# Attention begun on the first 512 rows: eight heads on four key blocks with their sums kept, the rest of norm, K and V made beside it

## Chip, cores, metric

One core of one Trainium2 chip. The metric is device time in microseconds (us) of the slowest core, here the only one; the figure quoted for a kernel is the median of its fast runs. "Span" is the time from the first to the last instruction in one profiled execution; it was 1.8 to 2.1 us below that execution's time in the profiled executions quoted here. The "granted clock" is the profile's record of TensorE's clock as a share of full speed (here 1.00 or, halved, 0.50), and PSUM is the memory that matmuls write to.

## The reference

Two layers; each is attention with 32 heads of 16 columns on 2048 rows of 512, then an MLP of width 1792, both with a norm ahead and a residual. Weights are the same in both layers. Inputs and output are bfloat16.

```python
def attention(x, wqkv, wo):                 # x: 1 x 2048 x 512, H = 32, Dh = 16
    q, k, v = split_heads(x @ wqkv)
    scores = einsum("bhqd,bhkd->bhqk", q, k) * Dh ** -0.5
    o = einsum("bhqk,bhkd->bhqd", softmax(scores), v)
    return merge_heads(o) @ wo

for layer in range(2):
    x = x + attention(layernorm(x), wqkv, wo)
    x = x + relu(layernorm(x) @ w1) @ w2
```

Softmax takes 2 x 32 x 2048 x 2048 exponentials. They bound the kernel.

## The kernel before

The program is written in slots. One slot is one set of scores (three blocks of 128 keys x 512 queries, "wide", 1536 columns), the exponential of them on ScalarE, and the product with V of an earlier slot. In some slots VectorE takes the third block over with integer and polynomial steps, so that ScalarE has a "narrow" exponential of 1024 columns. A segment is one lane of four heads (t, of 8) on one group of 512 query rows (j, of 4). All other matmuls (Q, K, V, output projection, MLP) are "fillings" put between, through one PSUM bank, with a model of the engines' times deciding where. Key blocks are 128 rows, so 16 of them make the sequence. The pieces of code below are cut and condensed.

The start: four rounds in a row before any exponential.

```python
for j in range(NQS):                        # four groups of 512 rows
    tag = ("ln1", 0, j)
    for i in range(TPC): ln_stats(tag, j, i)
    ln_rstd(tag)
    # ... j == 0: masks
    for i in range(TPC):
        ln_apply(tag, j, i)
        pt = ln_transpose(tag, i)
        nc.scalar.copy(out=xnT[j][:, :, i * P : (i + 1) * P], in_=pt)
    k_fin(0, 0, j, plain(k_mms(0, j)))
    # ... j == 0: the first Q
    for kb in range(j * TPC, (j + 1) * TPC):
        nc.scalar.copy(out=v_out(0, kb), in_=v_in(plain(v_mms(kb))))
```

The segments: layer 0 runs each segment over all 16 key blocks. Layer 1 already splits the segments of its first 512 rows, since the last rows of layer 0 come late: twelve key blocks with the sums stored, then the last four with the sums loaded.

```python
for j in range(NQS):
    for T in range(4): add_run(0, j, T, range(NKB), False, False)
for T in range(NACC // 2): add_run(1, 0, T, range(NKB - TPC), False, True)      # store
for T in range(NACC // 2): add_run(1, 0, T, range(NKB - TPC, NKB), True, False) # load
```

The end of a segment: the sums leave PSUM (`u`), and the reciprocal of the softmax denominators is made by three small transfers on one queue, so that VectorE computes 128x16 values and not 128x512.

```python
def copy():
    if sg["load"]: nc.vector.tensor_add(out=u[:], in0=acc[t], in1=ps_o[:])
    else:          nc.vector.tensor_copy(out=u[:], in_=ps_o[:])
    mark(("po",))                               # PSUM output bank is free
    if not last:
        nc.sync.dma_start(out=c[:], in_=sums)   # c<-u, 8 KB
        mark(("c", n), lag=2600.0)              # when the schedule counts on it
def recip():
    nc.vector.reciprocal(out=c[:], in_=c[:])
    nc.sync.dma_start(out=sums, in_=c[:])       # u<-c, 8 KB
    nc.sync.dma_start(out=r[:], in_=...)        # r<-u, 256 KB, 32 copies of each row
```

The tail uses seven PSUM banks in rotation, but the banks lie in three tiles, and a wait is for a whole tile:

```python
def bank():
    if not wide[0]: return ps_f[:]
    n = bank_no[0] % 7
    bank_no[0] += 1
    if n == 6: return ps_f[:]
    return ps_s[n // W][:, n % W, :]            # W = 3
```

The softmax here doesn't subtract the row's maximum and nothing guards it: scores larger than these inputs give would overflow.

Of the kernel before, what the change touches and what calls it, by code (L numbers as in the profile page):

```python
# [21 lines left out]
def kernel(  # L22
# [82 lines left out]
    xn2T = sb([P, NDC, QS], BF16, "xn2T")  # L105
    ht = [sb([P, QS], BF16, f"ht{ft}") for ft in range(NF)]
    ot = [sb([P, QS], BF16, f"ot{t}") for t in range(NT)]
# [3 lines left out]
    de = sb([P, 2, QS], BF16, "de")  # L111
    acc = [x[:, k, :] for x in [dm, dy] + dis for k in range(2)]
    ebuf = [sb([P, W, QS], BF16, f"e{n}") for n in range(NE)]
    qbuf = [[sb([P, QS], BF16, f"q{n}_{e}") for e in range(2)] for n in range(2)]
# [16 lines left out]
    wq_src = A_wqkv[:, :].rearrange("(c p) f -> p c f", p=P)  # L131
    for tt in range(4):
        nc.sync.dma_start(out=x_t[tt][:], in_=x_flat[tt * P : (tt + 1) * P, :])
    nc.scalar.dma_start(out=wqkv[:, :, D : 2 * D], in_=wq_src[:, :, D : 2 * D])
    nc.scalar.dma_start(out=wqkv[:, :, 2 * D : 3 * D], in_=wq_src[:, :, 2 * D : 3 * D])
    for tt in range(4, NTT):
        nc.sync.dma_start(out=x_t[tt][:], in_=x_flat[tt * P : (tt + 1) * P, :])
    nc.scalar.dma_start(out=wqkv[:, :, 0:D], in_=wq_src[:, :, 0:D])
    nc.sync.dma_start(out=wo[:], in_=A_wo[:, :].rearrange("(c p) f -> p c f", p=P))
    nc.sync.dma_start(out=w2[:], in_=B_w2[:, :].rearrange("(c p) f -> p c f", p=P))  # L140

    nc.gpsimd.memset(warm[:], 0.0)
    nc.scalar.activation(out=warm[:], in_=warm[:], func=ACTF.Exp)
    make_identity(nc, ident[:])
# [189 lines left out]

    def mm_group(mms, fin, makes, deps, per=2, cost=690, after=None):

        hold = {}
        pieces = []
        n = len(mms)
        for a in range(0, n, per):  # L340

            def piece(a=a):
                if a == 0:
                    hold["b"] = bank()
                b = hold["b"]
                for i in range(a, min(a + per, n)):
                    lhsT, rhs = mms[i]
                    nc.tensor.matmul(b, lhsT, rhs, start=(i == 0), stop=(i == n - 1))  # L348
                if a + per >= n:
                    put_evac(cost, lambda: fin(b))  # L350
                    if after:
                        after()

            pieces.append((min(per, n - a), piece))
        return group(pieces, makes, deps)
# [54 lines left out]
    def ln_rows(tag, j, i):  # L410
# [3 lines left out]
        prev = ln_seq[ln_seq.index(tag) - 1]  # L414
        task(750, lambda: ln_stats(tag, j, i), [("st", tag, i)])
        if i == TPC - 1:
# [105 lines left out]
    def h_group(l, j, ft, war):  # L522
        n = ((l * NQS + j) * NF + ft) % NW1

        def fin(b):
            if wide[0] and ft % 2:
                nc.scalar.activation(out=ht[ft][:], in_=b, func=ACTF.Relu)
            else:
                nc.vector.tensor_scalar(  # L529
                    out=ht[ft][:], in0=b, scalar1=0.0, scalar2=None, op0=ALU.max  # L530
                )
# [53 lines left out]

    def add_run(l, j, T, kbs, load, store):
        n = len(runs)
        runs.append((l, j, T))
        for e in range(2):
            segs.append(  # L590
                {
                    "l": l, "j": j, "t": 2 * T + e, "e": e, "T": T, "kbs": kbs, "n": n,
                    "load": load, "store": store, "begun": set(),
                }
            )

    for j in range(NQS):
        for T in range(4):
            add_run(0, j, T, range(NKB), False, False)
    early = range(NKB - TPC)  # L600
    late = range(NKB - TPC, NKB)
    for T in range(NACC // 2):
        add_run(1, 0, T, early, False, True)
    for T in range(NACC // 2):
        add_run(1, 0, T, late, True, False)
    for T in range(NACC // 2, 4):
        add_run(1, 0, T, range(NKB), False, False)
    for j in range(1, NQS):
        for T in range(4):
            add_run(1, j, T, range(NKB), False, False)  # L610

    norm_no = [0]

    def finish_segment(sg, last):
        l, j, t, e = sg["l"], sg["j"], sg["t"], sg["e"]
        if sg["store"]:
            musts.append(
                (690, now_pe[0] + PE_TO_DVE,
                 lambda: (nc.vector.tensor_copy(out=acc[t], in_=ps_o[:]), mark(("po",))))
            )  # L620
# [9 lines left out]
        def copy():  # L630
            if sg["load"]:
                nc.vector.tensor_add(out=u[:], in0=acc[t], in1=ps_o[:])  # L632
            else:
# [150 lines left out]

    for j in range(NQS):
        tag = ("ln1", 0, j)
        for i in range(TPC):
            ln_stats(tag, j, i)
        ln_rstd(tag)
        if j == 0:  # L790
            for e in range(2):
                nc.vector.tensor_reduce(
                    out=mask[e][:],
                    in_=ident[:].rearrange("p (g e d) -> p e g d", g=4, e=2)[:, e],
                    op=ALU.add, axis=mybir.AxisListType.XY,
                )
            for e in range(2):
                nc.vector.tensor_scalar(
                    out=qmask[e][:], in0=mask[e][:], scalar1=SCALE * LOG2E * UNIT, scalar2=None,
                    op0=ALU.mult,  # L800
                )
        for i in range(TPC):
            ln_apply(tag, j, i)
            pt = ln_transpose(tag, i)
            nc.scalar.copy(out=xnT[j][:, :, i * P : (i + 1) * P], in_=pt)  # L805
            mark(("xnT", tag, i))

        def plain(mms):
            b = bank()
            for i, (lhsT, rhs) in enumerate(mms):  # L810
                nc.tensor.matmul(b, lhsT, rhs, start=(i == 0), stop=(i == len(mms) - 1))  # L811
            return b

        k_fin(0, 0, j, plain(k_mms(0, j)))
        if j == 0:
            urgent.append(q_group(None, 0, 0, 0, 0))
            run_all()
        for kb in range(j * TPC, (j + 1) * TPC):
            nc.scalar.copy(out=v_out(0, kb), in_=v_in(plain(v_mms(kb))))
            mark(("v", 0, kb))  # L820
    for T in range(1, 4):
        work.extend(k_group(0, T, j) for j in range(NQS))
    for tag in [("ln1", 0, NQS - 1)]:
        assert ln_seq[-1] == tag

# [6 lines left out]
    recents = [[], []]  # L832
    exp_end = {-1: 0.0, 0: 0.0}
    pair_at = None
    now_dve[0] = 0.0
    while blocks:
# [16 lines left out]
        sg, kb, g = now[-1]  # L853
        pace = 3.0 if sg["store"] or sg["load"] else max(todo / max(rest - 6.0, 6.0), 0.5)
        owed[0] = min(owed[0] + pace, 6.0) if todo else 0.0
# [21 lines left out]
        half = None  # L877
        if len(now) == W and now[0][0] is sg and not (sg["load"] or sg["store"]):
            r = (kb * 4 + g - 2) // W
            if pair_at is not None:  # L880
                half = 1 if r == pair_at + 2 else None
            elif len(pairs) < 2:
                queued = sum(t["cost"] for t in dve_q if "chain" in t)
# [82 lines left out]
```

## Time and profile before

| | before |
|---|---|
| median of 3 runs | 1879.19 us (1876.68 to 1881.48) |
| profiled span, mean granted clock | 1876.4 us, 0.979 |
| until the first exponential | 67.9 us |
| exponentials on ScalarE | 1725.4 us in 1366 |
| idle of ScalarE before them | 14.5 us |
| after the last one (tail) | 68.6 us |

The four last rows add up to the span. That is the whole accounting: anything that is not in one of these four terms lies beside the exponentials and costs nothing. The lines that they come from are in the prediction.

### The profile page before, as it was taken

The numbers are of one execution on the slowest core, as the hardware profiler recorded it, in microseconds if no ns is written. First come the engines' busy times: TensorE is split into PE (matmuls) and PEld (weight loads), VectorE is DVE, ScalarE is ACT, GpSimd is POOL, SyncE is SP. The second block draws the span as 40 slices with busy tenths as digits, with TensorE's granted clock in tenths as the row PEclk, the third lists the DMA queues.
The fourth block names the chain that finished last, engine by engine and source line by source line (L and its number), as shares of the span: only waits on it lengthen the run. The fifth ranks groups of instructions, "written<-read, shape, count | busy, mean of one in ns | idle before, by whom it ended". The sixth has DMA issues, their size and how long they took to land.

```text
span 1876.4 us, 29319 instructions
## 1 busy us (share of the span) xinstructions
PE 1617.2 (86%) x12546; PEld 517.2 (28%) x12712; DVE 1244.0 (66%) x1864; ACT 1749.2 (93%) x1407; POOL 2.4 (0%) x35
## 2 busy tenths in 40 slices
PE   4788888899888998899899978888889888889966
PEld 2222222222222222222223222222222222222222
DVE  4677767868877786967642322786568768796672
ACT  2699999999999999999899998999999999999950
POOL 0000000000000000000000000000000000000000
PEclk8899999999999999999899998999999999999998
DMA  4000000110001100011001001011000110001101
GB/s 140 1 7 12 13 12 8 23 43 12 8 13 35 27 10 13 13 38 24 11 6 40 1 7 32 12 27 38 21 16 7 35 32 16 13 13 41 26 16 39
DMA packets 92742, 42.24 MB, mean 23 GB/s; under 512 B 76612, under 2 KB 84548, under 8 KB 92612
## 3 DMA queue, kind: packets, MB, share of 16 engines
q1 hardware_dynamic: 91028, 38.79, 9.1%
q8 instruction: 99, 1.62, 0.4%
q10 hardware_dynamic: 1584, 1.57, 0.2%
q14 instruction: 31, 0.25, 0.0%
HBM read 20.71 MB, written 2.10 MB: 12 GB/s over the span
## 4 chain that ended last, share of the span: by engine, by line
ACT 84%; PE 10%; DVE 4%; DMA 2%; issue 1%; SPq 0%; DVEq 0%
ACT e L894 83%; PE ps_s L871 3%; PE ps_o L685 2%; PE ps_f L348 2%; PE ps_s L348 2%; PE ps_s L811 1%; DMA c<-u 1%; DVE stats L367 0%; ACT xnT L805 0%; PE ps_s L404 0%; DMA r<-u 0%; DVE q L484 0%; DVE x L545 0%; DMA x<-in_A_x_dram 0%; DVE ht L529 0%
## 5 line engine op out<-in xcount | busy, mean ns | idle before, releaser
L894 ACT ACTIVATE e<-ps_s 128x1536 bf16<-128x1536 f32 (+1 forms) x1366 | 1725.4, 1552 | 14.5 <-PE ps_s L871 13.4
L871 PE MATMUL ps_s<-q,ktp 32*128 32x512 bf16 x6276 | 702.5, 384 | 170.2 <-ACT e L894 140.0
L685 PE MATMUL ps_o<-e,vaug 128*32 128x512 bf16 x3830 | 545.3, 393 | 7.2 <-DVE u L632 3.3
L871 PEld LDWEIGHTS <-ktp 32*128 32x128 bf16 x6276 | 224.9, 92 | 624.9 <-issue 548.1
L685 PEld LDWEIGHTS <-vaug 128*32 128x32 bf16 x4628 | 166.2, 93 | 455.6 <-issue 426.0
L726 DVE TENSOR_SCALAR di<-ps_s 128x512 int32<-128x512 f32 x266 | 182.9, 688 | 103.6 <-PE ps_s L871 101.2
L756 DVE SCALAR_TENSOR_TENSOR de<-dy,di 128x1024 bf16<-128x1024 f32 x133 | 162.6, 1223 | 7.2
L756 DVE SCALAR_TENSOR_TENSOR dy<-dm 128x1024 f32<-128x1024 f32 x133 | 162.5, 1222 | 2.9
L756 DVE SCALAR_TENSOR_TENSOR dy<-dy,dm 128x1024 f32<-128x1024 f32 x133 | 162.4, 1221 | 2.6
L529 DVE TENSOR_SCALAR ht<-ps_f 128x512 bf16<-128x512 f32 x99 | 68.2, 689 | 101.1 <-PE ps_f L348 100.6
L348 PE MATMUL ps_f<-w,ht 128*128 128x512 bf16 x365 | 110.1, 383 | 6.0 <-issue 4.8
L348 PE MATMUL ps_f<-xn2T,w 128*128 128x512 bf16 x353 | 107.8, 382 | 6.4 <-issue 3.0
L645 DVE SCALAR_TENSOR_TENSOR ot<-u,mask,r 128x512 bf16<-128x512 f32 (+1 forms) x67 | 48.1, 718 | 81.3 <-DMA r<-u 81.1
L685 PE MATMUL ps_o<-de,vaug 128*32 128x512 bf16 x532 | 94.6, 382 | 0.0
L750 DVE TENSOR_SCALAR di<-di 128x1024 int32<-128x1024 int32 x133 | 91.8, 690 | 2.9
L750 DVE TENSOR_SCALAR dm<-di 128x1024 int32<-128x1024 int32 x133 | 91.5, 688 | 1.5
L348 PE MATMUL ps_f<-xnT,wqkv 128*128 128x512 bf16 x210 | 67.2, 388 | 6.1 <-issue 4.5
L484 DVE TENSOR_SCALAR q<-ps_f,qmask 128x512 bf16<-128x512 f32 x70 | 50.2, 743 | 28.0 <-PE ps_f L348 27.5
L685 PE MATMUL ps_o<-di,vaug 128*32 128x512 bf16 x266 | 66.2, 391 | 0.0
L348 PE MATMUL ps_f<-wo,ot 128*128 128x512 bf16 x199 | 61.0, 384 | 1.6 <-issue 1.4
L634 DVE COPY u<-ps_o 128x512 f32<-128x512 f32 x56 | 38.6, 690 | 28.8 <-PE ps_o L685 28.4
L545 DVE TENSOR_TENSOR x<-x,ps_f 128x512 bf16<-128x512 bf16 x29 | 19.9, 685 | 54.6 <-PE ps_f L348 54.1
(67 smaller groups left out, 485.5 us busy)
## 6 DMA issues: line engine op xcount, KB each, us to landing
r<-u SPq DMA_DIRECT2D x63, 256.0 KB
w<-in_B_w_dram SPq DMA_DIRECT2D x112, 128.0 KB
x<-in_A_x_dram SPq DMA_DIRECT2D x16, 128.0 KB
out_dram<-x SPq DMA_DIRECT2D x16, 128.0 KB
w<-in_B_w_dram SPq DMA_DIRECT2D x1, 1792.0 KB
wqkv<-in_A_wqkv_dram ACTq DMA_DIRECT2D x3, 512.0 KB
c<-u SPq DMA_DIRECT2D x63, 8.0 KB
u<-c SPq DMA_DIRECT2D x63, 8.0 KB
```

The costliest lines, as they stand in the source:

```text
L348: nc.tensor.matmul(b, lhsT, rhs, start=(i == 0), stop=(i == n - 1))
L484: nc.vector.tensor_scalar(out=qbuf[n % 2][e][:], in0=b, scalar1=qmask[e][:, 0:1], scalar2=None, op0=ALU.mult,)
L529: nc.vector.tensor_scalar(out=ht[ft][:], in0=b, scalar1=0.0, scalar2=None, op0=ALU.max)
L545: nc.vector.tensor_add(out=x_t[tt][:], in0=x_t[tt][:], in1=b)
L634: nc.vector.tensor_copy(out=u[:], in_=ps_o[:])
L645: nc.vector.scalar_tensor_tensor(out=ot[t][:, a : a + w], in0=u[:, a : a + w], scalar=mask[e][:, 0:1], in1=r[:, a : a + w], op0=ALU.mult, ...
L685: nc.tensor.matmul(ps_o[32 * g : 32 * g + 32, :], vaug[sg["l"]][kb][:, 4 * sg["T"] + g, 2 * e : 2 * e + 32], rhs, start=g not in sg["begun ...
L726: first = nc.vector.tensor_scalar(out=di[:, half, :].bitcast(I32), in0=src, scalar1=EXP_BIAS, scalar2=0.0, op0=ALU.add, op1=ALU.max,)
L750: nc.vector.tensor_scalar(out=out[:].bitcast(I32), in0=di[:].bitcast(I32), scalar1=keep, scalar2=put, op0=ALU.bitwise_and, op1=ALU.bitwise_or,
L756: nc.vector.scalar_tensor_tensor(out=out[:], in0=x[:], scalar=c, in1=y[:], op0=ALU.add, op1=ALU.mult)
L871: nc.tensor.matmul(b[:, w, :], kt[32 * g : 32 * g + 32, kc : kc + P], qbuf[sg["n"] % 2][sg["e"]][32 * g : 32 * g + 32, :], start=True, sto ...
L894: ex = nc.scalar.activation(out=eb[:, :m, :], in_=b[:, :m, :], func=ACTF.Exp, scale=1.0 / (LOG2E * UNIT),)
```

## The change

Attention should begin as soon as the first 512 rows have their norm, K and V. Layer 0 gets the split that layer 1 has: all eight segments of the first 512 query rows go over the four key blocks that exist, with their sums stored in tiles that are free then; later the same eight segments go over the other twelve. The norm, transposes, K and V of the other 1536 rows become fillings. The first loads are reordered (x first, on two queues), idle matmuls are put ahead to have TensorE's clock up, no pairs go to VectorE until all sixteen K tiles of layer 0 exist, and fillings come in pieces of one matmul instead of two.

```diff
+    load_x(nc.sync, (0, 2))
+    load_x(nc.scalar, (1, 3))
+    nc.scalar.activation(out=warm[:], in_=warm[:], func=ACTF.Exp)
+    load_w(nc.sync, D)                     # K; then Q on scalar, x 4-7, V, x 8-15
...
-    def mm_group(mms, fin, makes, deps, per=2, cost=690, after=None):
+    def mm_group(mms, fin, makes, deps, per=1, cost=690, after=None):
...
+        early = range(TPC if l == 0 else NKB - TPC)
+        late = range(len(early), NKB)
+        sums = acc0 if l == 0 else acc
+            add_run(l, 0, T, early, store=sums)
...
+            add_run(l, 0, T, late, load=sums)
...
+    idle_matmuls(18)
+    # statistics, root, four transposes of the first 512 rows, one idle matmul after each,
+    # masks, three statistics of the next rows, K(0), Q(0), V(0), V(1); then:
+    work.extend(v_group(0, kb) for kb in range(2, TPC))
+    for j in range(1, NQS):
+        # ... ln_rows, k_group(0, j, 0), ln_groups, k_group(0, 0, j), v_groups as fillings
...
-            elif len(pairs) < 2:
+            elif len(pairs) < 2 and not any(key not in made for key in first_layer):
```

(Cut to its core; the rest renames buffers and sets the model's clock for the new start.)

## The prediction

> **What bounds the kernel now.** I read the page's busy shares first, then the instructions of ScalarE's one big group laid over time, then the timelines of the two ends.
>
> ```profile
> PE 1617.2 (86%) x12546; PEld 517.2 (28%) x12712; DVE 1244.0 (66%) x1864; ACT 1749.2 (93%) x1407; POOL 2.4 (0%) x35
> ACT  2699999999999999999899998999999999999950
> ```
>
> ScalarE is 93% busy, and its row of slices is 9 everywhere but at the two ends and, slightly, in the middle. The costliest groups say what it does:
>
> ```profile
> L894 ACT ACTIVATE e<-ps_s 128x1536 bf16<-128x1536 f32 (+1 forms) x1366 | 1725.4, 1552 | 14.5 <-PE ps_s L871 13.4
> L726 DVE TENSOR_SCALAR di<-ps_s 128x512 int32<-128x512 f32 x266 | 182.9, 688 | 103.6 <-PE ps_s L871 101.2
> ```
>
> Of 1749.2 us, 1725.4 are softmax exponentials, with only 14.5 us of idle before them. The second line is the first step of the exponentials VectorE takes over: 266 blocks of 128x512 in 133 pairs. Each such block shortens one ScalarE exponential from 1536 columns to 1024. The timelines of the ends:
>
> ```profile
> 3.04 0.69 DVE L367 BATCH_NORM_STATS2 stats<-x 128x6 f32<-128x512 bf16 x1 [3.04 <-DMA x<-in_A_x_dram]
> 5.00 0.69 DVE L367 BATCH_NORM_STATS2 stats<-x 128x6 f32<-128x512 bf16 x1 [1.05 <-DMA x<-in_A_x_dram]
> 6.77 0.69 DVE L367 BATCH_NORM_STATS2 stats<-x 128x6 f32<-128x512 bf16 x1 [0.86 <-DMA x<-in_A_x_dram]
> ...
> 15.97 1.87 PE L811 MATMUL ps_s<-xnT,wqkv 128*128 128x512 bf16 x4 [0.73 <-ACT xnT L805]
> ...
> 46.06 1.02 PE L811 MATMUL ps_s<-xnT,wqkv 128*128 128x512 bf16 x4 [0.67 <-ACT xnT L805]
> ...
> 67.89 7.91 ACT L894 ACTIVATE e<-ps_s 128x1024 bf16<-128x1024 f32 x7
> ```
>
> The first exponential begins at 67.89 us. Before it lie four serial rounds (one per 512 rows) of norm, transpose, K and V, in which ScalarE was busy only 19.7 us with copies. The last exponential ends at 1807.8, and 68.6 us of last output projection, norm and MLP follow. So the span is 67.9 + (1725.4 + 14.5) + 68.6 = 1876.4 us. The timed median, 1879.2, is 2.8 above that span.
>
> The idle 14.5 us matter for the rivals. Two stretches of the table of windows hold most of it (columns: stretch, length, busy PE, PEld, DVE, ACT, POOL with counts, granted clock, DMA):
>
> ```profile
> 904.00:908.00 4.00, 4.00 (x25) 0.74 (x22) 3.06 (x4) 2.77 (x3) 0.00 (x0) 0.50 0.02 4
> 1156.00:1160.00 4.00, 4.00 (x27) 0.74 (x24) 0.42 (x2) 2.99 (x3) 0.00 (x0) 0.50 0.19 39
> ```
>
> TensorE's clock is half there, and TensorE is full while ScalarE waits for scores. Just before, TensorE had stood for one VectorE copy of the output sums (2.9 us at 1150).
>
> **What the Trainium skill says.** "Perfetto Trace Analysis", section Identifying the Most-Contended Engine: for ScalarE, occupancy is a fair measure of how near the roofline is. The trace agrees: 100.00 busy in most 100 us stretches. "TensorE: Matmul & The Clock Gate", Part 1: The HAM clock gate: the clock is halved by default and released by roughly 3.4 us of activity; 512 columns then start every 215.7 ns, not 426.7. The trace agrees: four K matmuls took 1.87 us at 15.97 and 1.02 at 46.06. "Trainium Kernel Development and Optimization", section Key Constraints: queues of different engines share the same 16 DMA engines, so more queues save only issue time. The trace fits: with a 512 KB weight transfer issued at 0.73 beside them, the second and third x tiles came only at 5.0 and 6.8, while the engines moved about 380 GB/s.
>
> **The change, part by part.**
>
> *1. Earlier start.* Attention now begins when 512 rows have norm, K for T=0, Q and two V blocks. I walk its path with the durations above.
> - All four x tiles are issued first, on two queues. 512 KB at 380 GB/s is 1.4 us, so with the first at 3.0 none should hold VectorE. Statistics take about 0.79 us a tile back to back, ending near 6.3 (8.5 before).
> - The reciprocal root is 12 small operations of about 0.2 us, to 8.7.
> - Normalised rows, transposes and copies: the transposes still wait for the copy before them, since banks share a tile (the trace shows that wait, 0.67 us). Four rounds of 0.4 + 0.5 to 0.6 take it to 12.9. The 18 idle matmuls are there to have the clock full by then: 8 cold ones at 0.43 and 10 warm at 0.22 end near 7.
> - K 1.0, its copy on ScalarE 0.65, Q 1.0 (it waits for that copy): 15.6. VectorE has put the masks and three statistics of the next rows before Q's copies (0.55 + 2.4), so is free at 15.9. Two Q copies end at 17.3. V0 and V1 end on TensorE at the same time.
> - Scores 0.4, and ScalarE's copy of V1: first exponential at about 18.0.
>
> 67.9 - 18.0 = **49.9 us saved**. The 19.7 us of ScalarE copies before also leave (14 of 16 transposes' copies and 14 of 16 V copies go to VectorE or beside attention), but they lay inside those 67.9, so they are not counted again.
>
> *2. Exponentials given back.* The first runs (eight segments of four key blocks, 128 blocks) take no VectorE pairs, nor does any segment until all sixteen K tiles of layer 0 exist. The instruction order of the changed kernel has 1131 exponentials of 1536 columns and 234 of 1024, against 1099 and 266: 32 blocks return to ScalarE. In bins of 128 blocks the first two fall from 12 and 10 narrow ones to 0 and 2; the other 12 are lost here and there by the packing. The form means differ by 1637 - 1206 = 431 ns, so **+13.8 us** of ScalarE, all on the path.
>
> *3. Work beside attention.* The norm of 1536 rows, their transposes, K and 14 V blocks now run under the exponentials. A wide exponential starts every 1.343 us (14 of them in 18.91 us, the last lasting 1.45). TensorE per slot: scores and values about 0.22 each (row groups run at once), two switches near 0.1, and two to four filling matmuls of 0.22: 1.1 to 1.5 us. It just fits. VectorE from the first exponential to the last V copy sums to 47 us of instructions against 57 slots, 77 us: it fits. But two places do not:
> - Right after the start VectorE runs a statistic (0.8) and the root chain (2.4) before the next Q's two copies (1.4). The single filling bank is held meanwhile; V2 stands behind it in TensorE's order, before the values and scores of slot 4. Scores come near 23.4 where 22.1 was needed: 1.4 us.
> - Slots 53 to 58: transposes, K and four V blocks of the last rows are forced in a row, each through one bank and one VectorE copy: about 1 us for K, 1 for the V blocks.
>
> Any pause there may halve the clock, and a slot with two fillings then needs about 2 x 0.9 + 0.2 = 2.0 us, over 1.343, for several slots. I put 2.5 us on that. Together **+6 us** of idle.
>
> *4. The rest.* Four more Q groups and eight more hand-overs of sums fall on TensorE and VectorE, beside the exponentials. Smaller filling pieces (one matmul, not two) should not delay scores more than before. Layer 1 keeps its short runs, so I keep the 14.5 us and the 68.6 us tail.
>
> Sum: 18.0 + (1725.4 + 13.8) + (14.5 + 6.0) + 68.6 = 1846.3 us of span; plus 2.8 for the timed median: 1849, and I take **1848 us**, 1.7% less, as Part 1 may run a little shorter than my walk.
>
> **Rivals.**
> - *TensorE becomes the bound of the first 100 us.* For: 1.1 to 1.5 us of work per 1.343 us slot, one filling bank, and the half clock that followed hand-over pauses at 900 and 1150 now has eight more hand-overs to arise from. Against: clock was 1.00 in every 100 us stretch from 100 to 900. It would cost some 10 to 15 us more: about 1860.
> - *No added stalls, and smoother layer 1.* The smaller pieces and the altered statistic cost (860 for 750) look tuned. If the early stalls are 1 to 2 us and the half-clock stretches near 900 and 1150 lose half their 13 us, the time is about 1838, over 2% faster.
> - *The start is held by the weights or by a cold clock.* The Q weights are issued after the table load on ScalarE's queue. For: 2 MB of x and 1.5 MB of weights compete. Against: at 380 GB/s even all 3.6 MB are in by about 12, and Q's matmul is at 14.6. If the idle matmuls fail to warm it, K, Q and V lose about 0.9 us each: first exponential at 21, about 1851.
> - *VectorE loses nothing by offloading less and the returned blocks cost nothing.* That needs ScalarE to have slack; 100.00 busy speaks against. It would give 1834.
>
> **Range and chances.** Start is good to 2 us, the returned blocks to half a microsecond, early stalls to about 4, layer 1 to about 5; added as squares about 7 us, and 1.28 of that is 9. I widen upwards for cold-clock episodes: 1837 to 1860. The 2% line is 1841.6, almost one such spread below my value: faster 0.18, within 2% 0.81, slower 0.01.
>
> **What would show it.** First exponential at 16 to 20 us; x statistics back to back from about 3 us with no DMA waits; the group of exponentials with about 1739 us busy and about 20 us idle before them; the narrow form counted 234; no half clock beyond a few microseconds before 120; tail near 68.6. I am wrong if the idle before exponentials passes 30 or falls under 12, or if the first exponential is later than 22.

## The result, and the profile after

| | runs | median us |
|---|---|---|
| before, same comparison | 4 | 1878.15 |
| after | 4 | 1855.68 (1848.99 to 1862.37) |

The ratio is 0.9878, 95% interval 0.9838 to 0.9917: 1.2% less time, within the 2% line. Ratios here are the mean time of one kernel's fast runs over the mean of the other's fast runs of the same rounds, so they are not quite the ratio of the medians quoted. Executions over 1.5% slower than the fastest of the same kernel are left out of the means.

The page after, lines that answer to those of before:

```profile
PE 1660.1 (89%) x12509; PEld 521.9 (28%) x12509; DVE 1170.9 (63%) x1796; ACT 1749.7 (94%) x1380; POOL 2.4 (0%) x35
ACT  6999998999999999999999998999999999999940
L926 ACT ACTIVATE e<-ps_s 128x1536 bf16<-128x1536 f32 (+1 forms) x1366 | 1741.2, 1588 | 28.9 <-PE ps_s L903 27.9
L737 DVE TENSOR_SCALAR di<-ps_s 128x512 int32<-128x512 f32 x234 | 160.8, 688 | 101.2 <-PE ps_s L903 99.8
```

The first slice of ScalarE went from 2 to 6, the exponentials grew from 1725.4 to 1741.2 us, VectorE's share of them fell from 266 blocks to 234, and the idle before exponentials doubled, to 28.9 us.

Its timeline at the start (start, length, engine, line, operation, shapes, count, and in brackets the idle before and what ended it):

```profile
3.26 0.69 DVE L379 BATCH_NORM_STATS2 stats<-x 128x6 f32<-128x512 bf16 x1 [2.14 <-DMA x<-in_A_x_dram]
4.09 0.66 DVE L379 BATCH_NORM_STATS2 stats<-x 128x6 f32<-128x512 bf16 x1
...
13.26 1.02 PE L832 MATMUL ps_s<-xnT,wqkv 128*128 128x512 bf16 x4 [0.39 <-DVE mask L816]
...
18.22 4.14 ACT L926 ACTIVATE e<-ps_s 128x1536 bf16<-128x1536 f32 x3
23.80 9.51 ACT L926 ACTIVATE e<-ps_s 128x1536 bf16<-128x1536 f32 x7 [1.43 <-PE ps_s L903]
```

After the first tile no statistic waits for a transfer, K runs warm, the first exponential is at 18.22 us, and the fourth waits 1.43 us. The walk in the prediction had 18.0 and 1.4.

This profiled execution was the slowest of the four (1862.37 us). The other three were 5 to 13 us shorter, so one look is not enough to account for the kernel. The same kernel again as a control: 1852.7 us (1852.48 to 1853.85, 5 runs), ratio 0.9846 [0.9833, 0.9858]. (One run of the kernel before there took 3272.52 us; it counts as slow and is in no ratio.) The sum in four terms, us:

| term | before | predicted | control | first profile after |
|---|---|---|---|---|
| first exponential | 67.9 | 18.0 | 20.6 | 18.2 |
| exponentials | 1725.4 | 1739.2 | 1739.2 | 1741.2 |
| idle before them | 14.5 | 20.5 | 21.4 | 28.9 |
| tail | 68.6 | 68.6 | 70.7 | 72.2 |
| span | 1876.4 | 1846.3 | 1851.9 | 1860.6 |

The control's group line, for the second and third row:

```profile
L926 ACT ACTIVATE e<-ps_s 128x1536 bf16<-128x1536 f32 (+1 forms) x1366 | 1739.2, 1592 | 21.4 <-PE ps_s L903 20.6
```

The 21.4 us are all gaps before exponentials; 20.6 of them are waits for scores, and the split that follows is of these. Four questions follow. Why did the start reach 18.2 once and 20.6 in the control? Why is the tail longer, when nothing in it was changed? Which part of the change pays and which costs? And what are the 13.6 us of the control's idle that lie between 890 and 1210 us (6.3 lie before 130, 0.6 between), which the kernel before has too (12.7)?

### The profile page after: what moved, and what is told of

The parts are those of the page before. It is cut to its first block, busy times and chain, and to the rows that moved or that the text cites. A ratio compares the mean times of both kernels' runs of the same rounds, so it can differ in the third digit from the quotient of the medians.

```text
span 1860.6 us, 28967 instructions
## 1 busy us (share of the span) xinstructions
PE 1660.1 (89%) x12509; PEld 521.9 (28%) x12509; DVE 1170.9 (63%) x1796; ACT 1749.7 (94%) x1380; POOL 2.4 (0%) x35
## 4 chain that ended last, share of the span: by engine, by line
ACT 84%; PE 10%; DVE 3%; DMA 2%; issue 0%; SPq 0%; DVEq 0%
ACT e L926 84%; PE ps_s L903 4%; PE ps_o L696 2%; PE ps_s L360 2%; PE ps_f L360 1%; DMA c<-u 1%; DVE stats L379 0%; DMA r<-u 0%; DMA wqkv<-in_A_wqkv_dram 0%; DVE ht L542 0%; DVE q L497 0%; DVE vaug L490 0%; DVE ot L656 0%; DVE r L678 0%; DMA u<-c 0%
## 5 line engine op out<-in xcount | busy, mean ns | idle before, releaser
L926 ACT ACTIVATE e<-ps_s 128x1536 bf16<-128x1536 f32 (+1 forms) x1366 | 1741.2, 1588 | 28.9 <-PE ps_s L903 27.9
L737 DVE TENSOR_SCALAR di<-ps_s 128x512 int32<-128x512 f32 x234 | 160.8, 688 | 101.2 <-PE ps_s L903 99.8
L767 DVE SCALAR_TENSOR_TENSOR de<-dy,di 128x1024 bf16<-128x1024 f32 x117 | 143.1, 1223 | 8.9 <-PE ps_o L696 2.5
L767 DVE SCALAR_TENSOR_TENSOR dy<-dm 128x1024 f32<-128x1024 f32 x117 | 142.9, 1221 | 2.4
L767 DVE SCALAR_TENSOR_TENSOR dy<-dy,dm 128x1024 f32<-128x1024 f32 x117 | 142.8, 1220 | 2.1
L360 PE MATMUL ps_f<-xn2T,w 128*128 128x512 bf16 x400 | 122.5, 383 | 3.4 <-DVE ht L542 0.6
L360 PE MATMUL ps_f<-w,ht 128*128 128x512 bf16 x392 | 123.3, 385 | 0.5
L360 PE MATMUL ps_f<-xnT,wqkv 128*128 128x512 bf16 x280 | 88.8, 392 | 4.2 <-DVE vaug L490 1.4
L360 PEld LDWEIGHTS <-w 128*128 128x128 bf16 x448 | 36.2, 98 | 73.4 <-issue 59.3
L360 PEld LDWEIGHTS <-ht 128*128 128x128 bf16 x448 | 34.5, 97 | 70.1 <-issue 57.0
```

Of the source, the lines that this page charges most:

```text
L360: nc.tensor.matmul(b, lhsT, rhs, start=(i == 0), stop=(i == n - 1))
L737: first = nc.vector.tensor_scalar(out=di[:, half, :].bitcast(I32), in0=src, scalar1=EXP_BIAS, scalar2=0.0, op0=ALU.add, op1=ALU.max,)
L767: nc.vector.scalar_tensor_tensor(out=out[:], in0=x[:], scalar=c, in1=y[:], op0=ALU.add, op1=ALU.mult)
L926: ex = nc.scalar.activation(out=eb[:, :m, :], in_=b[:, :m, :], func=ACTF.Exp, scale=1.0 / (LOG2E * UNIT),)
```

## The experiments

Twelve kernels ran, on three chips; the kernel before ran beside them, with medians of 1881 to 1883 us. All results were correct. Unless said otherwise an edit is to the changed kernel. Where a first exponential, tail or idle is quoted, it is from the one profiled execution.

**1. The tail: one more turn of the banks.** In the kernel before, the program asks for a bank 37 times before the tail, 37 mod 7 = 2; after the change 8 times, 8 mod 7 = 1. Then the first two output projections fall into one PSUM tile. TensorE's timeline of the tail in the control, the changed kernel run again (as told above):

```profile
1793.17 5.17 PE L360 MATMUL ps_s<-wo,ot 128*128 128x512 bf16 x16 [3.73 <-DVE x L515]
```

The same stretch in this experiment:

```profile
1788.94 4.02 PE L360 MATMUL ps_s<-wo,ot 128*128 128x512 bf16 x9 [1.41 <-DVE ot L656]
1793.88 1.89 PE L360 MATMUL ps_s<-wo,ot 128*128 128x512 bf16 x8 [0.92 <-DVE x L515]
```

```diff
     wide[0] = True
+    bank_no[0] = 2
     run_all()
```

> Edit: before the tail the bank counter is set to 2, where the kernel before happened to stand; in the changed kernel it stands at 1. Theory (the tail grew from 68.6 to 72.2 us because the first two output projections now fall into banks of one tile, so the second waits for VectorE's addition of the first): from the end of the last exponential to the end of the span 68.6 us, within 0.5, and the time 3.6 us (0.2%) lower than the changed kernel. Rival (the tail is longer only because the clock was halved there): still about 72 us whenever the clock row of the tail is as low, and no wait for the addition removed.

Measured: 1851.32 us (1850.04 to 1861.52, 5 runs), ratio 0.9845 [0.9822, 0.9869]; tail 68.6 us. In the control the second projection stands 3.73 us until VectorE has added the first one to x (`DVE x L515`); with the edit nine matmuls go through in one stretch, and the wait is 0.92, as in the kernel before. The clock is halved for part of the tail in both, as before the change; its first half-clock stretch is 6.8 us with the edit and 10.2 in the control. So the control's extra 2.1 us of tail is what the rotation's phase cost. Experiments 9 and 12, with the same edit, have tails of 68.6 and 68.9. In time alone it is not seen: the ratios of this kernel and the control are 0.9845 and 0.9846. (The first profile of the changed kernel has the same wait of 3.73 and a tail of 72.2; its first half-clock stretch is 13.7 us, and the sixteen matmuls take 6.41 us, not 5.17.)

**2. No idle matmuls.**

```diff
     def idle_matmuls(n):
-        for _ in range(n):
+        for _ in range(0):
```

> Edit: no idle matmuls at the start (22 matmuls left out). Theory (they warm the clock for the start): the first exponential begins 2 to 3.5 us later than 18.2, with K, Q and V at 1.87 us per four matmuls instead of 1.02, and the time is 2 to 4 us higher than the changed kernel. Rival (warming is worth nothing, the path is set by VectorE's statistics and Q copies): first exponential within 1 us of 18.2.

Measured: 1853.23 us (1849.52 to 1853.71, 4 runs), ratio 0.9842 [0.9822, 0.9862]; first exponential at 20.54, K 1.87 us. The control, which has them, has the same. The control's timeline on TensorE:

```profile
1.19 5.61 PE L799 MATMUL ps_o<-e 128*128 128x512 bf16 x18 [1.19 <-DVE e L144]
9.80 0.40 PE L416 MATMUL ps_s<-ident,xn 128*128 128x128 bf16 x4 [3.00 <-DVE xn L407]
...
14.23 1.87 PE L832 MATMUL ps_s<-xnT,wqkv 128*128 128x512 bf16 x4 [0.18 <-DVE mask L816]
```

And two rows of the control's table of windows (stretch, length, busy PE, PEld, DVE, ACT, POOL with counts, granted clock, DMA):

```profile
10.00:12.00 2.00, 1.16 (x10) 0.43 (x7) 0.70 (x3) 0.59 (x1) 0.00 (x0) 0.80 0.98 325
12.00:14.00 2.00, 1.84 (x10) 1.03 (x10) 0.77 (x3) 0.59 (x1) 0.00 (x0) 0.50 0.68 214
```

The eighteen end at 6.8 us, TensorE rests 3.00 us, and the clock goes to half at about 11.2, 3 us before K. In the first profile of the changed kernel the same eighteen took 7.02 us and ended at 8.2, the rest was 1.24 us, and the clock stayed. So in the control the idle matmuls are worth nothing. The other kernels bear this out: of the ten profiled executions with eighteen idle matmuls, the seven with a rest of 2.26 to 3.53 us before the first transposes went to half clock by 12.1 us, and the three with 1.24, 1.88 and 2.01 us (the first profile and those of experiments 10 and 3) had K at 1.02 us. (A trap: the record of the clock starts late when a kernel begins cold. In experiment 2 it reads 1.00 from 14 to 16 us, though K took 1.87 us at 14.02.)

**3. Fillings in pieces of two matmuls, as before the change.**

```diff
-    def mm_group(mms, fin, makes, deps, per=1, cost=690, after=None):
+    def mm_group(mms, fin, makes, deps, per=2, cost=690, after=None):
```

> Edit: filling pieces of two matmuls again, not one. The build has 252 narrow exponentials where the changed kernel has 234, so 18 blocks go back to VectorE. Theory (the returned blocks cost 0.43 us each on ScalarE's path): ScalarE's exponentials are busy 7.7 us less, about 1733 us, and the time is about 8 us (0.4%) lower if idle stays equal. Rival (the one-matmul pieces pay for themselves by less waiting for scores): idle before the exponentials rises by as much or more, 37 us or over, and the time is equal or higher.

Measured: 1860.54 us (1858.25 to 1874.52, 6 runs), ratio 0.9902 [0.9873, 0.993]. Its group line, in its slowest run:

```profile
L926 ACT ACTIVATE e<-ps_s 128x1536 bf16<-128x1536 f32 (+1 forms) x1366 | 1738.1, 1530 | 45.1 <-PE ps_s L903 42.8
```

There are 252 narrow exponentials and not 234: eighteen of the 32 blocks given back are the price of the small pieces. They are worth it: on the same chip in the same rounds, pieces of two cost 0.6% (0.9902 against the 0.9842 and 0.9845 of experiments 2 and 1), for 19.9 us of idle between 130 and 890 us, where the control has 0.6.

**4. Scores repeated, to keep the clock up.** The program can issue the same scores again to keep TensorE at work; a constant says how much work per time is wanted.

```diff
-    FLOOR = 0.56
+    FLOOR = 2.0
```

> Edit: the score matmuls are repeated whenever there is room (up to three times), not only when the estimated activity falls under 0.56; 7680 score matmuls instead of 6099, and 242 narrow exponentials by the way (8 more). Theory (the idle beyond 20.5 us, and the spread of 13 us between executions, come from stretches of half clock that begin after a pause or a thin stretch of TensorE): few or no half-clock stretches between 20 and 1780 us, mean granted clock 0.98 or more, idle before exponentials under 15 us, spread between executions under 5 us, time about 1840. Rival (the added repeats themselves hold up the scores): no half clock, but idle before the exponentials stays at 25 us or more, and the time does not fall.

Measured: 1856.35 us (1855.36 to 1863.68, 4 runs), ratio 0.9861 [0.9839, 0.9883]. My theory fell: with 7680 score matmuls and not 6099 the clock was still at half for 41 us from about 1123 on, and the idle was 33.2 us (profiled in the slowest of the four runs). My reading is that repeats cannot run while TensorE stands for VectorE, and that at half clock they are themselves in the way; only the first half of that is seen in the traces, as the stretch again begins with TensorE standing, 3.56 us at 1122, for the addition to the sums.

**5. The control** (the changed kernel, unedited):

> The changed kernel unedited, as a control on the chip of the other runs of this batch. My sum with its measured terms (first exponential 18.2 to 20.6, exponentials 1739 to 1741, idle 21 to 29, tail 72.2) gives 1851 to 1863; single executions should spread by 10 us or more, with the mean granted clock falling from 0.98 to 0.966 as the time rises. If times spread without the clock, half-clock stretches are not what makes the spread.

Measured as told above. One expectation failed: the spread of 10 us or more did not come. The five runs lie within 1.4 us of each other, all at a mean clock of 0.975.

**6. Pairs allowed from the start.**

```diff
-            elif len(pairs) < 2 and not any(key not in made for key in first_layer):
+            elif len(pairs) < 2:
```

> Edit: VectorE pairs are allowed before all K tiles of layer 0 exist (the first short runs still take none). The build has 244 narrow exponentials where the changed kernel has 234. Theory (ScalarE pays 0.43 us for each returned block): exponentials busy 4.3 us less, about 1735 to 1737, and the time 4 us lower. Rival (the hold protects the K and V work of slots 43 to 80 on VectorE, and without it the scores wait): idle before the exponentials up to 130 us rises from 5 to 6 us to over 9, and the time is the same or higher.

Measured: 1860.57 us (1860.32 to 1862.64, 4 runs), ratio 0.9888 [0.9874, 0.9902], against 0.9846 for the control of the same rounds. Its group line:

```profile
L926 ACT ACTIVATE e<-ps_s 128x1536 bf16<-128x1536 f32 (+1 forms) x1366 | 1735.9, 1580 | 32.0 <-PE ps_s L903 31.2
```

Ten blocks come back to VectorE and ScalarE has 3.3 us less to do, but before 130 us it is idle for 17.0 us, where it was 6.3: which fits pairs that take VectorE from the copies that the first fillings wait for. The hold (no pairs before all K tiles exist) pays.

**7. The new start without the split.** Here the edit is to the kernel before: the new order of loads, the early zeroing, the masks moved behind the first rows and the 18 + 4 idle matmuls, with attention still begun after the fourth round.

```diff
+    load_x(nc.sync, (0, 2))
+    load_x(nc.scalar, (1, 3))
     ...
+    idle_matmuls(18)
     for j in range(NQS):
         ...
+            if j == 0:
+                idle_matmuls(1)
```

> The kernel before with the new start alone: loads in the new order on two queues, the earlier table load, idle matmuls, masks after the rows; all four rounds of norm, K and V still come before attention. Theory (the new start is worth a few microseconds, the splitting of attention the rest of the 49.7): first exponential at 61 to 65.5 instead of 67.9, and the time 3 to 7 us lower than before. Rival (the start order is most of the gain): first exponential under 55.

Measured: 1879.76 us (1878.16 to 1881.27, 4 runs), ratio 0.9988 [0.9974, 1.0002]; first exponential 65.09 (2.8 us sooner), given back as 1.1 of idle, 0.3 of exponentials and 1.4 of tail. The gain is the split's.

**8. The split with the old order of loads.**

```diff
-    load_x(nc.sync, (0, 2))
-    load_x(nc.scalar, (1, 3))
-    nc.scalar.activation(out=warm[:], in_=warm[:], func=ACTF.Exp)
-    load_w(nc.sync, D)
-    load_w(nc.scalar, 0)
-    load_x(nc.sync, (4, 5, 6, 7))
+    load_x(nc.sync, range(4))
+    load_w(nc.scalar, D)
     load_w(nc.scalar, 2 * D)
-    load_x(nc.sync, range(8, NTT))
+    load_x(nc.sync, range(4, NTT))
+    load_w(nc.scalar, 0)
+    nc.scalar.activation(out=warm[:], in_=warm[:], func=ACTF.Exp)
```

> The changed kernel with the loads in the old order (four x tiles on one queue, K, V, Q weights on the other, issued before the table load). Theory (the x tiles then wait behind weights again): the second and third statistics wait for x by about 1 us each, the first exponential comes about 2.5 us later than with the new order (20.5 to 23), time 2 to 3 us higher than the control. Rival (other parts of the path hide it): first exponential within 1 us of the control's.

Measured: 1857.76 us (1851.19 to 1867.55, 4 runs), ratio 0.988 [0.9842, 0.9917]; first exponential at 22.78, 2.1 us after the control's. The timeline shows where:

```profile
5.09 0.70 DVE L377 BATCH_NORM_STATS2 stats<-x 128x6 f32<-128x512 bf16 x1 [1.05 <-DMA x<-in_A_x_dram]
6.84 0.69 DVE L377 BATCH_NORM_STATS2 stats<-x 128x6 f32<-128x512 bf16 x1 [0.83 <-DMA x<-in_A_x_dram]
```

Statistics wait for x again, 1.05 + 0.83 us. The intervals of the two times overlap; only the profile settles it.

**9. Thirty idle matmuls, and the bank edit.** The number that reaches up to the transposes.

```diff
-    idle_matmuls(18)
+    idle_matmuls(30)
...
+    bank_no[0] = 2
     run_all()
```

> Edits at the two ends: 30 idle matmuls in place of 18, and the bank counter set to 2 before the tail. Theory (the 18 end near 6.8 us, and the 3 us of rest before the first transposes let the clock fall in most executions; the tail waits for an addition in the same tile): the 30 end near 9.5, no half clock between 8 and 18 us, first exponential at 18.2 to 18.9 instead of 20.6; tail about 2 us shorter than 70.7; together 4 us under the changed kernel's 1852.7 of the second batch. Rival (the clock falls for another reason, for instance because the transposes do not count as activity): first exponential still at 20.5, half clock still between 9 and 16 us, or the transposes are late because the idle matmuls are in their way.

Measured: 1853.8 us (1851.93 to 1856.39, 4 runs), ratio 0.9853 [0.9838, 0.9869]; tail 68.6; first exponential at 18.32.

```profile
1.18 8.45 PE L799 MATMUL ps_o<-e 128*128 128x512 bf16 x30 [1.18 <-DVE e L144]
...
13.35 1.02 PE L832 MATMUL ps_s<-xnT,wqkv 128*128 128x512 bf16 x4 [0.39 <-DVE mask L816]
```

The matmuls now end at 9.63, the transposes follow at once, and K is warm. The start is 2.3 us sooner, and the mechanism is shown. In time it brought little, where 4 us under the control were expected: about 49 us the clock went to half for 10 us in this execution, and idle before 130 us was 8.4 and not 6.3. One early gain was taken back by a later half clock.

**10. No small transfers where they are late.** What are the 13.6 us around 900 to 1210? The longest stretch in the control starts at 1117. First the timeline of the queue that issues the transfers, in the control:

```profile
1110.70 0.53 SPq L666 DMA_DIRECT2D r<-u  x1
1111.28 0.52 SPq L648 DMA_DIRECT2D c<-u  x1
```

The control's VectorE:

```profile
1117.60 0.25 DVE L664 RECIPROCAL c<-c 128x16 f32<-128x16 f32 x1 [7.17 <-DMA c<-u]
...
1118.35 1.40 DVE L497 TENSOR_SCALAR q<-ps_f,qmask 128x512 bf16<-128x512 f32 x2
1119.67 0.68 DVE L643 TENSOR_TENSOR u<-di,ps_o 128x512 f32<-128x512 f32 x1
```

Its TensorE:

```profile
1120.40 0.55 PE L696 MATMUL ps_o<-e,vaug 128*32 128x512 bf16 x4 [3.16 <-DVE u L643]
...
1121.97 1.46 PE L903 MATMUL ps_s<-q,ktp 32*128 32x512 bf16 x9
```

And its windows, with the columns given in experiment 2:

```profile
1116.00:1120.00 4.00, 0.83 (x8) 0.29 (x7) 2.40 (x5) 3.26 (x3) 0.00 (x0) 1.00 0.10 16
1124.00:1132.00 8.00, 8.00 (x51) 1.41 (x51) 1.52 (x3) 6.83 (x6) 0.00 (x0) 0.50 0.14 29
1140.00:1148.00 8.00, 8.00 (x46) 1.55 (x45) 6.70 (x8) 6.29 (x6) 0.00 (x0) 0.50 0.13 27
```

Read downwards. The 8 KB transfer `c<-u` is issued 0.58 us after the 256 KB transfer `r<-u` of the segment before, on the same queue, and the reciprocal that needs it starts 6.3 us later. The schedule had counted on 2.6 us and put the reciprocal next in VectorE's order. VectorE stands 7.17 us. Behind it in the order are the copies of Q and the addition of the next sums to `u`, which frees the PSUM output bank. TensorE stands 3.16 us for that addition, and its clock goes to half at about 1120. Then TensorE is busy 8.00 us of 8.00 at half clock: nine score matmuls take 1.46 us, while ScalarE takes a wide exponential every 1.343 us. ScalarE is busy only 6.83 and 6.29 of 8. This lasts 34 us and holds 8.7 us of the idle. The rest need not come first: in experiments 1 and 9 the clock falls at 1117.4 and 1117.6, only 0.2 us into the same rest, after 3.4 us in which TensorE was busy for 2.3.

That the 8 KB are late because of the 256 KB ahead of them can be read from the other late segments of the control. Where `r<-u` was issued 180, 5.9, 3.0, 0.58 and 0.57 us before `c<-u`, the reciprocal that waits for `c<-u` starts 1.85, 1.84, 3.93, 6.33 and 6.31 us after its issue. (To move `c<-u` to another queue would have tested this alone; it was not run.)

The edit takes the transfers away for the eight segments of layer 1 that load their sums, by making the reciprocals of all 128x512 on VectorE, as the last segment does in any case:

```diff
+        quick = l == 1 and sg["load"] is not None
+            mark(("u", n))
-            if not last:
+            if not last and not quick:
                 nc.sync.dma_start(out=c[:], in_=sums)
...
+        if quick:
+            task(650, shuffle, ...)               # spread the row of sums over its 32 partitions
+            for k in range(TPC):
+                task(900, lambda k=k: part(k * P), ...)   # reciprocal of 128 columns
+            task(700, lambda: mul(0, QS), ...)
```

> Edit: the eight short late segments of layer 1 take their reciprocals on VectorE itself (a shuffle and four pieces), not by the way of three small transfers. Theory (near 1120 VectorE stands 7 us for the transfer of the sums, copies the next sums late, TensorE stands 3 us, the clock halves for 34 us and ScalarE loses some 8 us): no 3 us wait of TensorE for VectorE's addition near 1120, the half-clock stretch there is gone or under 14 us, idle before exponentials between 890 and 1210 falls from 13.6 to about 6, time 6 to 8 us lower. Rival (the stretch comes from TensorE's own thin work there, or VectorE's 4.3 us more per segment makes it late in turn): half clock of 25 us or more remains and the idle stays over 11.

Measured: 1849.06 us (1835.13 to 1860.93, 6 runs), ratio 0.9839 [0.9808, 0.9869]. The group line of this experiment:

```profile
L940 ACT ACTIVATE e<-ps_s 128x1536 bf16<-128x1536 f32 (+1 forms) x1366 | 1736.3, 1609 | 7.4 <-PE ps_s L917 7.0
```

Its windows of the same stretch:

```profile
1116.00:1120.00 4.00, 3.38 (x37) 1.28 (x34) 3.92 (x7) 4.00 (x4) 0.00 (x0) 1.00 0.00 0
1124.00:1132.00 8.00, 6.56 (x62) 2.13 (x58) 7.84 (x10) 8.00 (x8) 0.00 (x0) 1.00 0.00 0
1140.00:1148.00 8.00, 7.24 (x60) 2.20 (x57) 3.59 (x6) 8.00 (x7) 0.00 (x0) 1.00 0.00 0
```

VectorE does more work there (four reciprocals take 3.39 us) and waits less; TensorE never waits for VectorE's addition between 1050 and 1200; the clock is full; ScalarE is busy throughout; the idle between 890 and 1210 us is 0. For the long stretch the cause is shown in this execution: it is the wait for the late 8 KB. Not all of the 13.6 us is the edit's. The control's other 4.9 us lie in half-clock stretches that begin at 1014.7 and 1072.7, before the first thing that the edit removes (the transfer issued at 1078.93); up to there the two traces show the same instructions in the same order. That these stretches are absent here, and in experiment 12, is therefore not explained by the edit. Nor is the warm start of this execution (first exponential at 18.52, after a rest of 1.88 us). But of the six executions only this one took 1835; the others took 1842 to 1861, at mean clocks of 0.984 down to 0.966. Something halves the clock in those elsewhere, and they were not profiled. The expected 6 to 8 us are not shown in time: the interval overlaps the control's (0.9833 to 0.9858).

**11. The rival: count on the transfer later.** If only the order is wrong, it is enough to tell the schedule the true delay.

```diff
-                mark(("c", n), lag=2600.0)
+                mark(("c", n), lag=7000.0)
```

> Edit: the schedule counts 7.0 us for the transfer of the sums, not 2.6 (the waits near 1120 show 5.8 to 7.1); the build has 240 narrow exponentials, 6 more than the changed kernel. Theory (VectorE is put in front of a transfer that has not landed, and everything behind it in its queue is late): VectorE's waits for that transfer fall from 37 us to under 15, the 3 us wait of TensorE near 1120 goes, idle between 890 and 1210 falls by 4 us or more, time 5 us or more lower. Rival (with the later estimate the segments are forced to wait for their normalisation in another place): idle between 890 and 1210 stays within 2 us of 13.6.

Measured: 1889.7 us (1881.52 to 1894.4, 6 runs), ratio 1.004 [1.0021, 1.0059]: slower than the kernel before. The waits of TensorE between 1050 and 1250 us (total, times, longest):

```profile
PE ps_o L696 <- DVE u L643: 14.0, 5, 4.2
PE ps_o L696 <- DVE u L645: 5.9, 2, 4.0
```

The waits of VectorE over the whole run:

```profile
DVE ot L656 <- DMA r<-u: 118.5, 26, 9.0
```

VectorE's waits for `c<-u` did fall, from 37.0 us to 1.2. But those for the third transfer of the chain, `r<-u`, rose from 81.9 to 118.5, and TensorE waits for VectorE to empty the output bank (the addition, L643, or the plain copy, L645) in seven places, 19.9 us in all (the control: once, 3.2 us). The idle between 890 and 1210 rose to 31.4 us, more than even the rival expected. Telling the schedule the true delay of one transfer is thus no cure, where taking the transfers off the path was.

**12. Both that worked: 9 and 10 together.**

> The edits of the two ends (30 idle matmuls, bank counter 2 in the tail) and of the direct reciprocals together. Theory (the gains lie in different stretches and add): first exponential at 18.3 to 19, tail 68.6, idle between 890 and 1210 under 3 us, the best execution near 1832, median 1845 or less, 1.9% or more under the kernel before; the times still fall and rise with the mean granted clock, by about 1 us for each 0.001. Rival (something took the place of the gain: the half clock moves to other stretches as it did in the slow executions of the direct kernel): median 1849 or more, with mean clock 0.975 or lower in most executions.

Measured: 1841.48 us, median of five fast runs (1830.52 to 1848.6), ratio 0.9788 [0.9758, 0.9819]: 2.1% less than before, unclear against the 2% line, and outside the interval of 9 alone (0.9838 to 0.9869), which ran on the same chip. It beats both kernels. A sixth run, 1861.52, was slow and is not counted. (It lies 1.7% above the fastest; 1860.93 of experiment 10, 1.4% above its fastest and at almost the same clock, is counted. With the sixth run the median would be 1843.97 and the ratio 0.9798, which is still outside that interval.) The page of its profiled execution:

```profile
PEclk9999999999999999999999999999999999999988
L940 ACT ACTIVATE e<-ps_s 128x1536 bf16<-128x1536 f32 (+1 forms) x1366 | 1735.8, 1612 | 7.0 <-PE ps_s L917 6.9
```

The clock is full until the tail but for 3.4 us near 50, and 18.7 + 1735.8 + 7.0 + 68.9 = 1830.4 us.

Over the fast runs of kernel 12 the time follows the mean clock (0.994 and 1830.52; 0.985 and 1841.48; 0.977 and 1848.6): about 1.06 us per 0.001 of mean clock, from the two ends. For kernel 10 a fit gives 0.97, for the changed kernel's first four runs 0.85. Since 0.001 of the mean is about 3.7 us at half clock, each microsecond at half clock costs some 0.27 us (the control's 34 us stretch, with 8.7 us of idle, gives 0.26). The spread between executions thus goes with how long the clock is halved. Why it is, in executions whose neighbours stay warm, is open.

## Why the prediction was right or wrong, point by point

The time was right (1848 predicted, 1855.68 measured, control 1852.7, both inside 1837 to 1860), and so was the class. Step by step:

- **Bound and accounting: right.** The four terms add to the span in every profile, and the time is the exponentials plus what stands around them. Two readings in the prediction were loose. The two windows that it shows hold 2.2 us of the 14.5, and it is the half-clock stretches around them, at 901 and 1154, that hold 9.4. And ScalarE is 100.00 busy in 8 of the 17 stretches of 100 us from 100 to 1800, though over 99.5 in 15.
- **Exponentials given back, +13.8 us: right, to a tenth partly by luck.** 1739.2 us in the control, but with the same 234 narrow ones it was 1735.8 to 1741.2 in other profiles. The reason given for twelve of the 32 blocks, "lost here and there by the packing", was incomplete: without the hold ten come back, and with pieces of two matmuls eighteen. The 1741.2 of the first profile, 2 us more with the same 234 narrow ones, fits its more numerous interruptions, since an exponential that follows another starts 1.343 us after it and one by itself takes 1.45. The 1736.3 and 1735.8 of experiments 10 and 12, with 7 us of idle, point the same way. That is argued and not tested.
- **Idle, 20.5 us: right in size for the control (21.4), too small for the first profile (28.9).** Of its parts, the stall of the fourth slot was 1.43 us against 1.4, the early term as a whole 6.3 and 5.2 against 6.0, and layer 1 kept its share (15.0 in the control after 130 us, against 14.5). The 6.3 are right partly by luck: the last rows' work cost 1.7 us near 98 to 102 (2 predicted), but 2.7 us lie at 52 to 56, where VectorE ran a root chain ahead of a V copy, the K block behind it came late and the prediction saw no stall; it had set 2.5 us aside for half clock at no certain place. The 7.5 us more of the first profile lie mainly in three stretches at half clock that the control does not have, near 133 to 144, 304 to 321 and 901 to 919 us.
- **The start, 18.0 us: the mis-sized term.** The step that failed is "the 18 idle matmuls are there to have the clock full by then". They did heat the clock and ended near 7 as I worked out; what I did not ask is what it does in the 3 us until the first transpose. The control measured 20.6, which is the third rival's 21. Experiment 2 shows the same 20.5 without them, experiment 9 shows 18.3 when they reach the transposes. The rest of the walk holds: with a warm clock the first profile gave 18.2. New loads are worth 2.1 us of it (experiment 8).
- **The tail, "I keep ... the 68.6 us tail": wrong by 2.1 us (3.6 in the first profile).** The code of the tail is unchanged, but its first PSUM bank is decided by how many banks were taken before, and that count changed from 37 to 8. Experiment 1 restores 68.6. It could have been counted in advance, by building both.
- **Rivals.** That TensorE becomes the bound of the first 100 us did not come true. That layer 1 becomes smoother did not either, but experiment 10 shows what it would have been worth: in its profiled run 13.6 us of idle are gone, 8.7 of them by the edit, where that rival had half of 13. That the returned blocks cost nothing is refuted by the 1739.2.
- **The 2.8 us from span to time** was 1.8 to 2.1: I had set a median of several runs against the span of one.

For the control: +2.6 (start) + 0.9 (idle) + 2.1 (tail) = 5.6 us, which is 1851.9 less 1846.3.

## What to carry to other kernels

When a serial prologue feeds a long stage bound by one engine, begin the stage on the part that is ready and keep partial sums: the first exponential came 47 to 50 us sooner, and the price was 14 us of work that the freed engine could no longer take over, and 5 to 6 us of stalls in the new first stage. When the clock depends on activity, warm-up work is worth something only if it reaches up to the real work (here a rest of 2.0 us was harmless and one of 2.3 us was not). An unchanged stage can change its time through a counter that it shares with a changed one (here the rotation of PSUM banks), and a small transfer that heads an engine's in-order work should not be queued behind a large one.

## What the Trainium skill lacked or had wrong

- "TensorE: Matmul & The Clock Gate", Part 1: The HAM clock gate: its table has the clock released after one busy window of about 3.4 us. The halved stretches do come in multiples of that (about 3.4, 10.2, 13.7, 17.1 and 34.1 us in these traces), but in the control TensorE was busy 8.00 of 8.00 us in 1124 to 1132 and 1140 to 1148, and the clock stayed at 0.50 for 34 us. The matmuls themselves were slow (nine scores in 1.46 us, 0.82 at full clock), so it is not the record that is at fault. The work there was mostly scores on 32 of 128 rows and products into 32 columns; whether that counts as less activity, the page does not say and no run here tested.
- The same table puts the fall after an idle window of about 3.4 us. Shorter rests went before the fall here: 3.16 us (ended at 1120.40, half clock from about 1120.5), and at the start of six executions 2.26 to 3.00 us (in the control 3.00, ended at 9.80, half clock from about 11.2). Rests of 1.24, 1.88 and 2.01 us at the same place in the program were not followed by it. Nor is a long rest needed. In the five traces that lack no matmul record (the first profile and experiments 9 to 12) TensorE was busy at most 2.3 of the 3.4 us before every fall; at 1015.2 in experiment 9 it was 2.15 us, with no rest over 0.7 us. (Some stretches as thin passed without a fall.)
- The same page says that the window runs freely, so that the number of cold matmuls varies from run to run; the trace agrees, the eighteen idle ones took 5.5 to 7.0 us in ten executions. The page puts the cost of that ramp under 1% of a kernel. It has no figure for how far executions of one kernel lie apart when the clock also falls later on: here fast executions of one kernel (experiment 10) went from 1835 to 1861 us at mean clocks from 0.991 to 0.966, about 1 us per 0.001.
- "SBUF — State Buffer", section The DMA setup-cost knee: a transfer costs roughly 2 us however small. Alone that is near what the trace shows (8 KB `u<-c` issued at 1108.90, the next transfer of the chain, which waits for it, issued at 1110.70: 1.8 us). For 8 KB issued 0.58 us behind 256 KB on the same queue it was 6.3 us. The section has no figure for a small transfer behind a large one.
